# K of two heads as one transfer of 65536-byte rows, in a two-layer decode step with a KV cache of 16384 keys

## The chip, the cores and the metric

The kernel runs on one core of one Trainium2 chip. The metric is the device time of one execution in microseconds, lower is better. A core has five engines, each with its own instruction queue: TensorE (PE, with the weight load PEld shown apart), VectorE (DVE), ScalarE (ACT), GpSimd (POOL) and SyncE (SP). 16 DMA engines move data between the memory of the chip (DRAM) and the on-chip memory of 128 partitions. Matmuls write to a separate accumulator memory in banks (PSUM).

## The reference

Two times the same layer, one token for each of two batch rows: attention over a cache with 32 heads a row, 16384 keys, head size 128, then a small MLP with shifted channel groups. All inputs are bf16.

```python
def _A_ref(x, k_cache, v_cache, wq, wo):
    q = (x @ wq).reshape(B, Sq, H, Dh).transpose(0, 2, 1, 3)
    scores = jnp.einsum("bhqd,bhkd->bhqk", q, k_cache) * (Dh ** -0.5)
    p = _softmax(scores, axis=-1)
    o = jnp.einsum("bhqk,bhkd->bhqd", p, v_cache)
    return o.transpose(0, 2, 1, 3).reshape(B, Sq, H * Dh) @ wo
...
x = x + _A_ref(_layernorm(x), A_k_cache, A_v_cache, A_wq, A_wo)
x = x + _B_ref(_layernorm(x), B_w1, B_w2, B_w3, B_w4)
...
```

The last two lines run twice, with the same weights and the same cache. There are 2 x 32 = 64 heads, counted through as u = 0 to 63. K and V of a head are 16384 x 128 numbers of 2 bytes, 4 MiB each; a layer reads 64 of each.

## The kernel before, in words

**Memory.** K and V live in one tensor, `mem`, of six slots (`NSLOT`) of 32768 bytes a partition (`TILE`). A head's K fills one slot: partition p holds 128 keys in a row, so that the slot is 128 blocks, each with one key of every partition. A planner (`plan_all`, L516) writes down all transfers of the whole program in one order, each with its place in `mem`. `pump` (L289) hands the next one to SP as soon as all cells of its place are free; `used` (L1281) releases a place when its last reader is done. SP thus holds one list of transfers (issued at L101), and each waits at the head of the list for the release of its own place; all that are issued run one behind the other through the same DMA queue.

**What is transferred.** K comes head by head, 128 rows of 32768 bytes (`plan_tile`, L433). V of two heads comes as one transfer of 128 rows of 65536 bytes (`plan_pair`, L445): partitions 0 to 63 hold head u, partitions 64 to 127 head u + 1, in two neighbouring slots. In the loop of layer 0, K of the first head of a pair goes to slot 0, of the second to slot 2, and V of the pair to slots 4 and 5.

**One head.** A head's scores need each key times q. Half of the 128 blocks go by TensorE: in chunks of eight blocks, PE transposes them (L1298, `transposes`) into one of four PSUM tiles `tps`, ACT copies the chunk to one of three tiles `kt` (L1314, `evacuate`), and PE multiplies the eight blocks with the column of q (L1328, `scores`), two chunks behind. The other half goes by VectorE in four groups of 16 blocks: a multiply with q spread over the partitions (L1348) and a sum over the 128 elements (L1354), together `dots` (L1340). q is spread by a diagonal matrix (DVE, L1259), a matmul (PE, L1263) and a copy (ACT, L1266). Then the softmax: the maximum on DVE (L1363 to L1368), over the partitions on POOL (L1370), the scaling and two exponentials on ACT (L1379, L1382, L1385).

**One pair.** As V holds two heads, p of both heads is spread to V's layout, `both`, by two matmuls a head with a selecting matrix (L1418, `spread_p`) and a copy (L1424). Then 256 matmuls of a V block with two columns of `both` (L1455, `pv_pair`) give the outputs of both heads; ACT keeps them (L1459), and this releases the V place.

**Loops.** Each engine has its own hardware loop, made by `Graph._turn` (L235) from the instructions of the first turns: waits are rebased by a fixed step a turn (L265). A turn is one pair, two heads one after the other. Layer 0 loops over heads 1 to 60 (30 turns), layer 1 over 58 heads (29 turns); the heads ahead and behind are written out. A column that changes with the turn (the head's column of q or of the sums) is computed in a register from the turn's number:

```python
emit_op(eng, o, None if o.col is None else turn * (ops[first + n + i].col - o.col) + o.col)
```

All tiles of K and V are at the same places in every turn, so their addresses are constants. POOL tells PE and DVE that a transfer has landed (`relay`, L81 and L205).

**Between the layers** the output projection, the MLP and the next layer's q use the weights, which the planner puts in places left free; K of the last two heads of layer 0 stays in `mem`, transposed, for layer 1, which therefore starts with these heads. `turn` (L1109) and `park` (L1126) transpose blocks for that between other steps.

Of the kernel before, what the change touches and what calls it, by code (L numbers as in the profile page):

```python
# [5 lines left out]
ALU = mybir.AluOpType  # L6
# [10 lines left out]
class Op:  # L17


    __slots__ = ("eng", "fn", "deps", "waits", "needed", "own", "val", "sem", "sig", "col", "pos", "know", "relay", "told")  # L20

    def __init__(self, eng, fn, sig=None, col=None):
        self.eng, self.fn, self.sig, self.col = eng, fn, sig, col
# [9 lines left out]
class Graph:  # L33
# [44 lines left out]
    def op(self, eng, fn, reads=(), writes=(), sig=None, col=None):  # L78
        return self._add(Op(eng, fn, sig, col), reads, writes)
# [54 lines left out]
    def emit(self):  # L134
# [15 lines left out]
        for e in self.LOOPED:  # L150
            ops = self.ops[e]
            for first, (n, turns) in self.loops[e].items():
                for i in range(first, first + n):
# [8 lines left out]
                    if same[0].col is not None:  # L162
                        step = same[1].col - same[0].col
                        assert all(o.col == same[0].col + t * step for t, o in enumerate(same)), [o.col for o in same]
        done = {e: nc.alloc_semaphore(f"done_{e}") for e in self.ENGS if e != "sync"}
# [37 lines left out]
        def emit_op(eng, o, col=None):  # L203
# [3 lines left out]
            ins = o.fn(eng) if o.col is None else o.fn(eng, o.col if col is None else col)  # L207
# [27 lines left out]
    def _turn(self, eng, ops, first, n, turns, taken, wait, needs, emit_op, handle):  # L235
# [22 lines left out]
        with self.nc.Fori(0, turns, 1, engines=OrderedEngineSet([me]), head_slot={me: 0}) as turn:  # L258
            seen = {}
            for i in range(n):  # L260
                wait(eng, rel[i], seen)
                o = ops[first + i]
                emit_op(eng, o, None if o.col is None else turn * (ops[first + n + i].col - o.col) + o.col)
# [68 lines left out]
class KB:  # L332
# [8 lines left out]
    NS = 3  # L341
    DB = 16
    PB = 32
# [3 lines left out]
    ENTER = (1, 3)  # L347
    LEAVE = (61, 61)
    TURNS = {("w3", 0): 1, ("w3", 1): 1, ("w3", 2): 1, ("w4", 1): 1, ("w4", 3): 1, ("w4", 6): 1, ("w4", 8): 1,
             ("wq", 0): 1, ("wq", 1): 1, ("wq", 2): 1}  # L350

    def __init__(self, nc, A_x, K, V, wq, wo, w1, w2, w3, w4, out):
# [20 lines left out]
        self.chunk = 0  # L373
# [3 lines left out]
    def _alloc(self):  # L377
# [6 lines left out]
        self.same = sb("same", [128, 4, 128], BF16)  # L384
        self.ones_bf, self.ident, *self.sel = (self.same[:, i, :] for i in range(4))
        self.ones_f = sb("ones_f", [128, 1], FP32)
        self.diag = sb("diag", [128, 128], BF16)
        both = sb("both", [128, 4 * self.NB], BF16)
        self.both = both[:, :].rearrange("p (k c) -> p k c", k=2)
        self.qb = [both[:, 0:128]] + [sb(f"qb{i}", [128, 128], BF16) for i in range(1, self.NS)]  # L390
        self.p = [both[:, 128:128 + self.NB]] + [sb(f"p{i}", [128, self.NB], BF16) for i in range(1, self.NS)]
        self.both_keys = [("qb", 0), ("p", 0), ("p2", 0), "both"]
        self.s_dve = [sb(f"s_dve{i}", [128, 2 * (self.BP - self.PB)], FP32) for i in range(self.NS)]
        self.q_f = sb("q_f", [128, U], FP32)
        self.q_col = sb("q_col", [128, self.NS], BF16)
# [49 lines left out]
    def plan_pair(self, u, slot):  # L445

        v = self.V.rearrange("b h s d -> (b h s d)")
        n = self.NB * 128 * 128
        self.store.plan(("w", u, 0, 2 * self.NB), "pair", slot * self.TILE, 2 * self.TILE,
                        [(lambda m: m, v[u * n:(u + 2) * n].rearrange("(p x) -> p x", p=128))])  # L450
# [65 lines left out]
    def plan_all(self):  # L516
# [9 lines left out]
        third = U - self.CARRY - 1  # L526
# [6 lines left out]
        for t, u, slot in (("k", third, 1), ("k", third + 1, 3), ("v", third, 4), ("k", third + 2, 5),  # L533
# [1048 lines left out]
```

## Time and profile before

| what | value |
|---|---|
| runs of the kernel before | 2545.34, 2546.11, 2546.92 us (median 2546.11) |
| span of the profiled execution, its only own time | 2543.9 us |
| runs' median less that span | 2.2 us |
| bytes moved by the data queue | 1092.39 MB |
| mean rate over the span | 430 GB/s |

How to read the profile. Times are in microseconds from the start of the span. L1298 is line 1298 of the kernel. A row of the timeline or of the groups names the line, the engine, the operation, what it writes and reads (`out<-in`), and how often (`x8`); in square brackets stands how long the engine was idle before it and what ended that (`<-issue`: nothing that the profile shows). A row of the chain of waits is a start, a length and what ran; a row of waits is who waited, for whom, how long in all, how often, and the longest. An engine's name with a q (`PEldq`, `SPq`) is its sequencer: register, branch, semaphore and DMA-issuing instructions, which aren't counted as busy. The granted TensorE clock is a share of full speed.

### The profile page before, as it was taken

What the parts mean: (1) busy time and instruction counts of PE and PEld (TensorE: products, weight loads), DVE (VectorE), ACT (ScalarE), POOL (GpSimd) and SP (SyncE); (2) the same over time, 40 slices, a digit from 0 to 9 for tenths busy, and PEclk for the clock granted to TensorE, in tenths of its full rate; (3) what the DMA queues carried; (4) which work ended last, traced back from release to release, by engine and by line L of the source; (5) the groups of instructions that cost most, each with busy time, mean ns of one, the idle gap of its engine ahead of it and who ended that gap; (6) DMA issues with size and microseconds to landing.
All of it is one profiled execution on the core that took longest, in us unless ns stands there. A gap on an engine that the chain in (4) does not pass through costs nothing.

```text
span 2543.9 us, 75560 instructions
## 1 busy us (share of the span) xinstructions
PE 1588.5 (62%) x34642; PEld 1520.1 (60%) x34642; DVE 1875.3 (74%) x1811; ACT 1250.8 (49%) x2114; POOL 109.6 (4%) x154
## 2 busy tenths in 40 slices
PE   3656666566566566565776656656656666566566
PEld 3555656566565565565765656656556566566566
DVE  5787787777877877877748687787787787777884
ACT  3454555554544544545535455454454555554553
POOL 0000000000000000000000000000000000000000
PEclk8666665565656656666656566566666565665665
DMA  9999999999999999999999999999999999999999
GB/s 414 424 437 429 434 438 430 428 442 424 434 433 432 432 437 428 436 435 426 418 413 432 434 429 437 429 431 439 425 435 433 431 436 433 428 437 430 432 431 383
DMA packets 38432, 1093.19 MB, mean 430 GB/s; under 512 B 4196, under 2 KB 5352, under 8 KB 11496
## 3 DMA queue, kind: packets, MB, share of 16 engines
q1 hardware_dynamic: 38376, 1092.39, 99.9%
q8 instruction: 41, 0.67, 0.1%
q14 instruction: 15, 0.12, 0.0%
HBM read 1092.37 MB, written 0.00 MB: 429 GB/s over the span
## 4 chain that ended last, share of the span: by engine, by line
DMA 60%; DVE 27%; PE 7%; issue 4%; ACT 1%; POOL 0%; SPq 0%; POOLq 0%; DVEq 0%; ACTq 0%
DMA mem<-in_A_k_cache_dram 57%; DVE s_dve L1354 17%; DVE prod L1348 9%; PE tps L1298 3%; DMA mem<-in_B_w_dram 1%; DMA mem<-in_A_v_cache_dram 1%; PE mps L1482 1%; PE sps L1328 1%; PE sps L1263 1%; DVE diag L1259 1%; ACT mem L1314 0%; PE mps L897 0%; PE mps L1455 0%; DMA mem<-in_A_wq_dram 0%; DMA mem<-in_A_wo_dram 0%
## 5 line engine op out<-in xcount | busy, mean ns | idle before, releaser
L1354 DVE TENSOR_REDUCE s_dve<-prod 128x16 f32<-128x2048 bf16 x504 | 1151.1, 2284 | 13.3
L1314 ACT ACTIVATE kt<-tps 128x1024 bf16<-128x1024 bf16 x992 | 966.5, 1029 | 171.8 <-PE tps L1298 159.9
L1348 DVE TENSOR_TENSOR prod<-mem,qb 128x2048 bf16<-128x2048 bf16 x492 | 602.1, 1224 | 524.5 <-POOLq L205 490.6
L1298 PE MATMUL tps<-same,mem 128*128 128x128 bf16 x8192 | 910.7, 285 | 31.3 <-issue 24.6
L1298 PEld LDWEIGHTS tps<-same,mem 128*128 128x128 bf16 x8192 | 730.8, 130 | 37.2 <-issue 30.2
L1455 PEld LDWEIGHTS mps<-both,mem 128*128 128x128 bf16 x15104 | 407.5, 103 | 48.2 <-ACT both L1424 43.2
L1455 PE MATMUL mps<-both,mem 128*128 128x2 bf16 x15104 | 412.5, 165 | 32.6 <-ACT both L1424 27.8
L1328 PE MATMUL sps<-q_col,kt 128*128 128x1 bf16 x7936 | 364.6, 168 | 53.6 <-ACT kt L1314 44.9
L1328 PEld LDWEIGHTS sps<-q_col,kt 128*128 128x128 bf16 x7936 | 351.7, 108 | 74.2 <-ACT kt L1314 69.6
L1418 PE MATMUL sps<-p,same 128*128 128x128 bf16 x236 | 46.3, 299 | 481.2 <-ACT p L1385 481.2
L1418 PEld LDWEIGHTS sps<-p,same 128*128 128x128 bf16 x236 | 15.6, 111 | 491.2 <-ACT p L1385 491.2
L1263 PE MATMUL sps<-diag,same 128*128 128x128 bf16 x126 | 36.0, 286 | 286.4 <-DVE diag L1259 284.6
L1370 POOL PARTITION_ALL_REDUCE mx<-mx x128 | 106.5, 832 | 2366.3 <-DVE mx L1368 2259.0
L1459 ACT ACTIVATE o_acc<-mps 128x2 f32 x59 | 10.2, 172 | 383.7 <-PE mps L1455 383.7
L1263 PEld LDWEIGHTS sps<-diag,same 128*128 128x128 bf16 x126 | 13.1, 104 | 296.8 <-DVE diag L1259 290.1
L1379 ACT ACTIVATE mx<-mx 128x1 f32<-128x1 f32 x128 | 26.2, 205 | 332.1 <-POOL mx L1370 332.0
L1266 ACT ACTIVATE qb<-sps 128x128 bf16<-128x128 f32 x123 | 33.8, 275 | 228.1 <-PE sps L1263 228.1
L1424 ACT ACTIVATE both<-sps 64x256 bf16<-64x256 f32 x118 | 44.6, 378 | 57.2 <-PE sps L1418 57.2
L1365 DVE TENSOR_REDUCE mx<-sps 128x1 f32<-128x64 f32 x128 | 28.2, 220 | 23.2 <-PE sps L1328 23.1
L1382 ACT ACTIVATE p<-s_dve,mx 128x64 bf16<-128x64 f32 x123 | 42.8, 348 | 4.0
L1314 ACT ACTIVATE mem<-tps 128x1024 bf16<-128x1024 bf16 x32 | 31.3, 1044 | 18.1 <-PE tps L1298 16.0
L1430 ACT ACTIVATE l<-ls 128x1 f32 (+1 forms) x120 | 35.3, 294 | 9.0
(131 smaller groups left out, 460.5 us busy)
## 6 DMA issues: line engine op xcount, KB each, us to landing
mem<-in_A_k_cache_dram SPq DMA_DIRECT2D x124, 4096.0 KB, 24.0
mem<-in_A_v_cache_dram SPq DMA_DIRECT2D x5, 4096.0 KB, 29.7
mem<-in_B_w_dram SPq DMA_DIRECT2D x21, 576.0 KB, 7.8
mem<-in_B_w_dram SPq DMA_DIRECT2D x7, 1152.0 KB, 32.7
mem<-in_A_v_cache_dram SPq DMA_DIRECT2D x3, 2048.0 KB, 36.9
mem<-in_A_wq_dram SPq DMA_DIRECT2D x10, 512.0 KB, 6.5
mem<-in_A_wo_dram SPq DMA_DIRECT2D x8, 576.0 KB, 18.4
mem<-in_A_wq_dram SPq DMA_DIRECT2D x4, 1024.0 KB, 8.0
```

The source lines that it names most:

```text
L1263: self.pe(lambda pe: pe.matmul(qps, lhsT=self.ones_bf[:, :], rhs=self.diag[:, :], start=True, stop=True, skip_group_check=True), reads=["o ...
L1298: ins = pe.transpose(self.tps[t][:, j * 128:(j + 1) * 128], buf[:, j * 128:(j + 1) * 128], self.ident[:, :])
L1314: self.act(lambda e: e.activation(out=out, in_=self.tps[t][:, :], func=ACT.Copy), reads=[("tps", t)], writes=keys, sig=("evac", c, t, k))
L1328: ins = pe.matmul(self.sps[sp][:, c * self.CH + j:c * self.CH + j + 1], lhsT=buf[:, j * 128:(j + 1) * 128], rhs=self.q_col[:, sp:sp + 1], ...
L1348: self.dv(lambda e: e.tensor_tensor(out=prod, in0=buf.rearrange("p (j d) -> p j d", d=128), in1=qbc, op=ALU.mult), reads=[("qb", r)] + key ...
L1354: self.dv(lambda e: e.tensor_reduce(out=sd[:, c0:c0 + DB], in_=prod, axis=AX.X, op=ALU.add), reads=["prod"], writes=[("s_dve", r)], sig=(" ...
L1370: self.pool(lambda e: e.partition_all_reduce(mx[3], mx[2], channels=128, reduce_op=ROP.max), reads=[("mx2", i), "cleared"], writes=[("mx3" ...
L1382: self.act(lambda e: e.activation(out=p[:, n:self.NB], in_=self.s_dve[i][:, 0:self.NB - n], func=ACT.Exp, bias=mx[4], scale=self.scale, ac ...
L1418: ins = pe.matmul(out[:, h * n:(h + 1) * n], lhsT=lhsT, rhs=self.p[i][:, :], start=True, stop=True, skip_group_check=True)
L1424: self.act(lambda e: e.activation(out=self.both[lo:hi, k, :], in_=out[lo:hi, :], func=ACT.Copy), reads=[("sps", 0), ("qps", 0)], writes=se ...
L1430: self.act(lambda e, c: e.activation(out=self.l[:, bass.ds(c, 1)], in_=self.ls[:, 0, i:i + 1], func=ACT.Identity, bias=self.ls[:, 1, i:i + ...
L1455: ins = pe.matmul(self.mps[:, 448:450], lhsT=buf[:, b * 128:(b + 1) * 128], rhs=self.both[:, :, col], start=b == 0, stop=b == 2 * self.NB ...
```

## The change

K of two heads is now planned as one transfer too, with the layout of V. `plan_pair` takes K or V:

```diff
-    def plan_pair(self, u, slot):
-        v = self.V.rearrange("b h s d -> (b h s d)")
+    def plan_pair(self, t, u, slot, cuts=()):
+        v = (self.K if t == "kp" else self.V).rearrange("b h s d -> (b h s d)")
...
-        self.plan_tile("k", 0, 1)
+        self.plan_tile("k", 0, 2)
         self.plan_tile("v", 0, 3)
-        for u in range(1, third, 2):
-            self.plan_tile("k", u, 0)
-            self.plan_tile("k", u + 1, 2)
-            self.plan_pair(u, 4)
...
+        place = lambda i: 0 if i % 2 else 2
+        self.plan_pair("kp", o[1], place(1))
+        for i in range(2, n + 1):
+            self.plan_pair("kp", o[2 * i - 1], place(i))
+            self.plan_pair("vp", o[2 * i - 3], 4)
```

The K places alternate: pair 1 in slots 0 and 1, pair 2 in slots 2 and 3, and so on; V pairs are always in slots 4 and 5. The order of the queue is K1, K2, V1, K3, V2, K4 and so on (Ki and Vi: pair i). There are 30 pairs in layer 0 and 29 in layer 1 (`PAIRS`); the first of each layer is written out, the others are the turns of the loop (29 and 28).

Since the place alternates, an operation can have an address that depends on the turn's parity. `Graph._turn` puts it into a register, and the operation adds its own offset:

```diff
+                if o.alt is not None:
+                    k = (o.alt, then.alt)
+                    if k not in flips:
+                        lo, d = min(k), abs(k[1] - k[0])
+                        flips[k] = self.nc.snap(((turn + (1 if k[0] > lo else 0)) % 2) * d + lo,
+                                                engines=OrderedEngineSet([me]))
+                    alt = flips[k]
...
+    def pair_transposes(self, l, u, k, c, at):
...
+                ins = pe.transpose(self.tps[t][:, j * 128:(j + 1) * 128],
+                                   self.mem[:, bass.ds(base + (c * self.CH + j) * 128, 128)], self.ident[:, :])
```

The same is done for the multiplies of `pair_dots`. A turn (`pair`) now is:

```diff
+    def pair(self, l, u, k, prev):
+        self.landed("kp", u, both=True)
+        pend = []
+        n = self.NB // self.CH
+        for c in range(n):
+            at, self.chunk = self.chunk, self.chunk + 1
+            self.pair_transposes(l, u, k, c, at)
+            spot = self.kt_spot(at)
+            self.evacuate(at, spot)
+            pend.append((c, spot))
+            if len(pend) > self.LEAD:
+                self.pair_scores(*pend.pop(0))
+            if c % 2 == 0:
+                self.pair_dots(l, u, k, c // 2)
+            if prev is not None and c == self.MID:
+                self.landed("vp", prev)
+            if prev is not None and self.MID <= c < self.MID + 2:
+                for g in range(2):
+                    self.pv_pair_part(l, prev, 2 * (c - self.MID) + g)
+            if prev is not None and c == self.MID + 1:
+                self.keep_pair(l, prev)
+        for c, spot in pend:
+            self.pair_scores(c, spot)
+        self.pair_max()
+        self.q_turn(u + 2)
+        self.pair_exp(u)
+        for nm in self.store.pieces("kp", u):
+            self.store.release(nm)
```

So 16 chunks a pair are transposed (128 of the pair's 256 blocks), `pair_scores` multiplies each block with two columns (q of both heads), and eight groups of 16 blocks go by DVE (`pair_dots`). The scores of a pair are in one PSUM bank and one tile `s_dve`, with a head in each half of the partitions. `pair_max` takes the maximum of each half (five DVE operations, one all-reduce of two columns on POOL); `pair_exp` writes the exponentials straight into `both`: two scalings, four exponentials and two kept sums on ACT. The last kept sum also stands as the last reader of the K place, which is released there. `spread_p` is gone, and so is the diagonal: q is spread by two matmuls with a repeated column of q (`rows_of_q`). PV of the previous pair (`pv_pair_part`, four parts of 64 matmuls) comes inside the pair, after chunks 12 and 13 (`MID` = 12), instead of at its end.

Around the loops: the heads not in pairs (one ahead in layer 0, three behind it in each layer) run through `single`, with the same steps as before but all DVE groups in the second half of the blocks. Layer 1 takes the carried heads in the order 61, 62, 63 and then 0 to 60. The last head of layer 0 takes its chunks in the order 5, 6, 7, 3, 4, 0, 1, 2, so that its last key chunks stay where they were transposed (`kt` and `tps`) for layer 1, in place of `park`. The bytes loaded are the same.

More of the change, by code (lines that the diff above doesn't have):

```diff
@@ L1083, in attention @@
[L1083 to L1086 removed]
+            self.q_row(o[0], 0, 2)
+            self.q_turn(o[1], None)
+            self.single(o[0], 0, 2)
+            self.softmax_max(o[0], 0, 2)
+            self.softmax_exp(o[0], 0, 2)
+            self.pv(l, o[0], 0)
+        self.pair(l, o[at(1)], 0, None)
+        first = self.g.mark()
+        self.base = self.chunk
+        for i in range(2, n + 1):
+            self.pair(l, o[at(i)], (i - 1) % 2, o[at(i - 1)])
```

785 lines of the change are left out of this document (357 added, 428 removed).

## The prediction

> **What bounds the kernel now.** I read the page's head first, for the resource that never rests.
>
> ```profile
> span 2543.9 us, 75560 instructions
> ...
> PE 1588.5 (62%) x34642; PEld 1520.1 (60%) x34642; DVE 1875.3 (74%) x1811; ACT 1250.8 (49%) x2114; POOL 109.6 (4%) x154
> ...
> q1 hardware_dynamic: 38376, 1092.39, 99.9%
> ```
>
> The transfers fill 99.9% of the span; no engine passes 74%. Who waits for whom comes next, from two answers on waits: that of SyncE's queue and that of all engines.
>
> ```profile
> SPq L101 <- PE sps L1328: 1577.9, 120, 41.9
> SPq L101 <- ACT o_acc L1459: 683.3, 59, 37.5
> ```
>
> ```profile
> DVE prod L1348 <- POOLq L205: 490.6, 58, 9.8
> ```
>
> SP issues each transfer as soon as its place is released and runs ahead of the DMA engines. VectorE waits for the landing of K in every turn: 490.6/58 = 8.5 us a turn. The stream of K and V is the bound, and compute has slack. How much, the windows show: four that reach from the first packet of one transfer to that of the next kind (V pair, K and K, V pair, K and K), then one whole turn. Columns: window, its length, busy time of PE, PEld, DVE, ACT, POOL, TensorE's granted clock, DMA share, GB/s.
>
> ```profile
> 598.59:617.95 19.36, 8.29 (x134) 8.11 (x132) 18.97 (x16) 9.80 (x16) 1.31 (x1) 0.66 1.01 438
> 617.95:637.38 19.43, 15.84 (x397) 15.12 (x394) 10.32 (x12) 9.76 (x19) 0.35 (x1) 0.55 1.00 430
> 637.38:656.72 19.34, 7.72 (x124) 7.46 (x125) 18.95 (x16) 9.49 (x16) 1.31 (x1) 0.71 1.00 434
> 656.72:676.15 19.43, 15.66 (x397) 14.64 (x395) 10.32 (x12) 9.75 (x19) 0.35 (x1) 0.58 0.99 427
> 591.30:630.08 38.78, 24.31 (x523) 23.54 (x521) 29.29 (x26) 19.52 (x33) 1.66 (x2) 0.59 1.00 433
> ```
>
> A turn of two heads is 38.78 us, the time of 16.78 MB at 433 GB/s. In it PE is busy for 24.31 us and DVE for 29.29. The chain of waits gives the pieces.
>
> ```profile
> 4.63 22.79 DMA mem<-in_A_k_cache_dram
> ...
> 591.32 1.24 DVE prod L1348
> 592.58 2.30 DVE s_dve L1354
> 594.90 1.24 DVE prod L1348
> ...
> 603.80 0.85 PE tps L1298 x8
> 604.65 0.20 PE sps L1328 x8
> ```
>
> One dot group costs DVE 594.90 - 591.32 = 3.58 us, eight of them 28.6; one transpose 0.85/8 = 0.106 us.
>
> **The change, part by part.**
>
> *K as one transfer of 65536-byte rows.* Bytes stay. The windows price it: the V pair, which has this form already, takes 19.34 to 19.36 us, the same bytes as two K transfers 19.43. So 0.07 to 0.09 us a pair, I take 0.08; with 30 + 29 pairs 4.7 us less (4.1 to 5.3). The windows' GB/s stand farther apart (438 and 434 against 430 and 427), but a window's edge cuts packets, and one packet of 65536 B is 0.8% of it; the lengths count. As the stream is 99.9% full, this is all that can be gained.
>
> *Dots, scores, softmax.* Eight dot groups a turn as before, so DVE keeps 28.6 us; 128 transposes, 16 evacuations and 256 PV matmuls stay too. The timeline at a turn's end has the rest:
>
> ```profile
> 621.00 0.22 DVE L1365 TENSOR_REDUCE mx<-sps 128x1 f32<-128x64 f32 x1 [0.28 <-PE sps L1328]
> 621.26 0.16 DVE L1368 TENSOR_TENSOR mx<-mx 128x1 f32<-128x1 f32 x1
> ...
> 621.51 0.35 POOL L1370 PARTITION_ALL_REDUCE mx<-mx  x1 [6.78 <-DVE mx L1368]
> 621.90 0.20 ACT L1379 ACTIVATE mx<-mx 128x1 f32<-128x1 f32 x1 [1.36 <-POOL mx L1370]
> 622.13 0.35 ACT L1382 ACTIVATE p<-s_dve,mx 128x64 bf16<-128x64 f32 x1
> ...
> 622.92 0.39 PE L1418 MATMUL sps<-p,same 128*128 128x128 bf16 x2 [1.96 <-ACT p L1385]
> 623.35 0.38 ACT L1424 ACTIVATE both<-sps 64x256 bf16<-64x256 f32 x1 [0.48 <-PE sps L1418]
> 623.75 0.72 ACT L1430 ACTIVATE l<-ls 128x1 f32 x2
> ...
> 623.78 6.99 PE L1455 MATMUL mps<-both,mem 128*128 128x2 bf16 x256 [0.47 <-ACT both L1424]
> ```
>
> Gone: twice the spread (0.39 on PE, 0.38 on ACT), the diagonal and one all-reduce of two. New at the pair's end: five DVE steps (about 1.0 us), one all-reduce (0.35), two scalings (0.4), four exponentials (1.4), two sums kept (0.72): 3.9 us from the last dot to the release of the K place. PE's next pair waits there after two chunks, because the scores have one bank. All of it lies beside the stream as long as a turn of compute stays under 38.7 us: DVE 28.6 + 1.0, then 2.9 for the rest, is 32.5. It costs nothing while 6 us of cover last.
>
> *Addresses from a register.* The place alternates between turns, so each of the 128 transposes, and each of the eight multiplies, gets its K address from a register. No row of before shows a register-addressed transpose. Nearest rows: the loop's own register and semaphore instructions on PE's sequencer (all of them, then three in a window of one back edge; minimum, median, maximum ns, first and last start):
>
> ```profile
> L258 PEldq ALU_OP  x59: 36/36/42, 92.6 to 2464.2; - x59
> ...
> L265 PEldq EVENT_SEMAPHORE  x3: 51/51/51, 591.4 to 591.7; - x3
> ```
>
> Three semaphore instructions of 51 ns start over 0.3 us, 0.15 apart. Scaled by 36/51, a register operation holds the sequencer for 0.106 us. A load and its matmul pass in 6.99/256 = 0.027. Lower bound of a transpose: the 0.106 of today, with the register work hidden ahead of the array. Upper: 0.15 + 0.027 = 0.18; if load and matmul are both slowed, or two operations are needed, above 0.2. I take 0.106 + 0.027 = 0.133, nearest to the ALU row. PE's turn then is 128 x 0.133 = 17.0, scores 16 x 0.20 = 3.2, PV 7.0, and about 6 for the pair's end (3.9 plus the last evacuations, 1.03 each): 33 us, under 38.7. PE becomes the bound at (38.7 - 16.2)/128 = 0.176 us a transpose. The eight on DVE are below 8 x 0.15 = 1.2 us and inside the slack.
>
> The Trainium skill speaks against this part: "TensorE: Matmul & The Clock Gate", section "Step-by-step: what each phase is for", says that a matmul not handled by the hardware decoder takes the sequencer about 62 ns. No run here shows whether a register address has that effect; 0.027 us for a PV pair says that plain ones don't. By it, as an estimate, a transpose would be 0.106 + 0.124 = 0.23 us and the second rival below would hold.
>
> *The queue at each layer's start.* K of pair i+2 waits for the end of pair i; V of pair i waits for PV of pair i-1, which now stands after chunk 12 of 16 of pair i. In the steady turn the V place is free some 10 us before its slot in the queue. Not at pair 2, where the loops start. Rows: entry of the first loop on DVE and ACT, and of the second on PE.
>
> ```profile
> 50.32 1.23 DVE L1348 TENSOR_TENSOR prod<-mem,qb 128x2048 bf16<-128x2048 bf16 x1 [6.49 <-issue]
> ...
> 54.61 1.94 ACT L1314 ACTIVATE kt<-tps 128x1024 bf16<-128x1024 bf16 x2 [5.24 <-PE tps L1298]
> ```
>
> ```profile
> 1349.76 1.46 PE L1298 MATMUL tps<-same,mem 128*128 128x128 bf16 x12 [4.97 <-issue]
> ```
>
> Layer 0: the first K lands at 4.63 + 22.79 = 27.4; V of that head 9.7 later; then pair K1, K2, V1, K3 at 19.35 each: K1 at 56.5, K3 ends at 114.5. Pair 1 computes from 56.6: 28.6 of dots, about 1 of gaps, 3.9 of end: 90. ACT's entry (5.2): 95. Then a chunk each 8 x 0.133 + 0.25 = 1.31 us: chunk 12 at 111, PV in two halves with a chunk between 8.3, o kept and V2 issued: 120, first bytes about 1 later. The stream stands for 121 - 114.5, about 6.5, and with the evacuations of chunks 0 and 1 behind the stall, 8 us. Bounds: nothing, if the entry is not waited for and a chunk stays at 1.1; 13 at 0.18 a transpose. Layer 1 is built alike, with a costlier entry on PE: 9. Both are paid once; after them the queue has its slack again.
>
> *The rest* (q rows made without the diagonal, tiles kept where they are transposed, layer order) changes engines with slack, beside the stream: nothing, at most 1 us either way.
>
> Sum on the profiled execution: 2543.9 - 4.7 + 8 + 9 = 2556.2; the median of the runs is 2.2 above that span, so **2558.4**.
>
> **Rivals.**
>
> *The start holes are covered (not slower).* Register work hides in the 0.106 us and the entry stalls fall into waits for K2: V2 is issued before 113.5, the stream stays full, and only the 4.7 remain: 2541.4 (2540.8 to 2542). It decides at whether PV of pair 1 ends before K3's last packet. For it: 24.31 us of PE in 38.78. Against: the 5.24 and 6.49 us rows.
>
> *PE's sequencer becomes the bound.* From 0.176 us a transpose on, the turn follows PE. At 0.20: 16.2 + 25.6 = 41.8, 3.1 over, in 29 + 28 looped turns 177 us: 2558.4 + 177 = 2735; at 0.18 2587; at 0.23, 2950. For it: 0.15 us between sequencer instructions, 128 of them new. Against: a sequencer may run ahead of the array while PE waits.
>
> *The rows bring nothing* (the DMA engines already hide what lies between packets; the 0.08 us is K's own place in the memory): the holes alone, 2563.
>
> *A fixed price per transfer falls away.* If each transfer's end cost 2 us of the stream, 59 fewer would give 118: 2428. Against it: 19.43 for two K and 19.35 for one V; an end costs 0.08. The rule is that of the Trainium skill, "SBUF — State Buffer", section "The DMA setup-cost knee", where every transfer pays about 2 us and larger ones are advised; by those two rows the trace doesn't bear it out for transfers queued back to back.
>
> **How the numbers follow.** Forecast 0.42 (2548 to 2580), covered 0.24, PE-bound 0.27, no gain 0.05, fixed price 0.02. A measurement of this kernel can tell about 0.2%, 5.1 us. Faster than 2541.0: half of the covered case and more, and the fixed price: 0.16. Within: the rest of the covered case and the lower end of the forecast, 0.15. Slower: 0.69. The range, 2539 to 2730, leaves out the fixed price, a little below, and PE-bound turns over 0.2 us a transpose. The forecast's own range is 2548 to 2580.
>
> **What would show it.** Right: V-pair issues 38.69 us apart instead of 38.78; the DMA tenths full except for one hole of 5 to 12 us near 115 us and one behind the layer change; DVE still waiting about 6 us a turn for K; transposes in chunks of 8 over 1.0 to 1.1 us; register rows on PE, 128 a turn. Wrong: DMA share under 98% all along with DVE or ACT waiting for PE (second rival); no hole (first); windows of K still 19.43 long (third). The forecast falls most easily with the one number that no row shows, a register-addressed transpose.

## The result and the profile after

| | before | after |
|---|---|---|
| median of the runs | 2546.48 us (2545.34 to 2546.92, 4 runs) | 2561.65 us (2559.45 to 2563.38, 4 runs) |
| span of the profiled execution | 2543.9 us | 2561.1 us |
| ratio, 95% interval | | 1.0059 (1.0044 to 1.0073) |

The change makes the kernel slower by 15.2 us; 2558.4 was forecast. The page of the kernel after, in the rows that answer to those shown of before:

```profile
span 2561.1 us, 82046 instructions
...
PE 1629.7 (64%) x34370; PEld 1472.1 (57%) x34370; DVE 1881.2 (73%) x1550; ACT 1255.4 (49%) x1944; POOL 31.1 (1%) x95
...
DMA  9899999999999999999999999999999999999999
GB/s 412 379 441 427 438 430 437 431 428 440 426 441 427 441 427 440 428 439 428 378 390 423 412 426 440 428 440 428 438 430 435 433 430 438 426 442 426 442 424 387
...
q1 hardware_dynamic: 30024, 1092.39, 99.2%
```

The same bytes, the queue 99.2% full instead of 99.9%, and three places where the rate falls under that of before: the second slice of 64 us (379, before 424), the twentieth and twenty-first, where the layers meet (378 and 390, before 418 and 413), and the twenty-third, where the loop of layer 1 starts (412, before 434). In the loops nothing is lost. SP's rows in the timeline of the kernel after (start, length, what is issued) give the steady turn from V pair to V pair:

```profile
344.37 0.33 SPq L101 DMA_DIRECT2D mem<-in_A_v_cache_dram  x1
...
383.07 0.33 SPq L101 DMA_DIRECT2D mem<-in_A_v_cache_dram  x1
```

383.07 - 344.37 = 38.70 us, against 38.78 before. The answer on waits shows that VectorE still waits for K in nearly every turn, 395.1/55 = 7.2 us each time:

```profile
DVE prod L1309 <- POOLq L206: 395.1, 55, 14.3
```

Where the loss sits is seen best by bytes. From the records of all packets I worked out the time at which each trace had moved a given number of megabytes, and took before from it. A number that grows down a column is time that the stream lost there, one that shrinks is time won. (e11, whose turns are longer, is not in the table.)

| trace | 45 MB | 60 MB | 520 MB | 575 MB | 650 MB | 1050 MB | 1092 MB |
|---|---|---|---|---|---|---|---|
| (place) | start | behind pair 2 | end of loop 0 | layer change over | behind pair 2 | end of loop 1 | end |
| after | -0.6 | 7.0 | 5.1 | 14.3 | 19.2 | 17.3 | 17.8 |
| e1 | -0.5 | 1.8 | 0.1 | 6.0 | 9.1 | 7.2 | 8.2 |
| e2 | -0.4 | -0.2 | 0.0 | 9.3 | 11.9 | 9.9 | 12.9 |
| e3 | -0.4 | 7.2 | 7.2 | 15.7 | 21.0 | 20.8 | 22.0 |
| e4 | -0.6 | 5.3 | 3.7 | 7.5 | 9.9 | 7.9 | 9.7 |
| e5 | -0.6 | 5.8 | 4.1 | 14.3 | 15.6 | 13.7 | 18.1 |
| e6 | -0.6 | 6.8 | 4.6 | 14.5 | 19.3 | 17.5 | 17.8 |
| e7 | -0.6 | 8.6 | 6.7 | 15.1 | 21.8 | 19.9 | 22.2 |
| e8 | -0.6 | -0.4 | -2.3 | 8.4 | 8.4 | 6.5 | 11.4 |
| e9 | -0.5 | 6.7 | 4.5 | 14.0 | 19.0 | 17.1 | 17.2 |
| e10 | -0.7 | -0.5 | -2.4 | 6.8 | 6.7 | 4.8 | 4.9 |
| e12 | -0.6 | -0.4 | -2.3 | 1.4 | 1.8 | -0.1 | 0.0 |

The row "after" is the whole story: 7.6 us lost at the start of layer 0, 1.9 won back in its loop, 9.2 lost at the layer change (0.9 near 1243 us, 5.4 near 1275, 3 where layer 1's first loads begin), 4.9 at the start of layer 1, 1.9 won back.

Each row is one execution, the profiled one, and that is not always a typical one: e1's took 2552.84 us (five runs of 2552.84 to 2560.77, median 2557.23), e2's 2557.76 (eleven runs of 2551.28 to 2557.76, median 2554.36). And the layer change costs between 3.8 us (e4) and 10.2 (e5) in versions whose instructions there are the same as in the kernel after. So a row places a loss, but two rows that differ by two or three microseconds show no difference by themselves.

Three windows of the kernel after show it as rate (the last columns are TensorE's clock, DMA share and GB/s; 433 is full):

```profile
100.00:130.00 30.00, 23.53 (x486) 20.69 (x485) 22.53 (x19) 17.04 (x29) 0.35 (x1) 0.61 0.76 319
...
1240.00:1280.00 40.00, 29.02 (x757) 27.80 (x758) 16.44 (x16) 14.40 (x23) 0.50 (x2) 0.59 0.88 353
1400.00:1420.00 20.00, 12.62 (x290) 11.19 (x286) 16.89 (x15) 6.52 (x18) 0.37 (x1) 0.50 0.81 333
```

The hole of layer 0 in the timeline of the kernel after (idle time before an instruction and its releaser in brackets):

```profile
89.79 0.60 ACT L1351 ACTIVATE l<-mq 64x1 f32<-64x1 f32 x2
90.41 0.33 SPq L101 DMA_DIRECT2D mem<-in_A_k_cache_dram  x1
...
95.73 12.95 ACT L1386 ACTIVATE kt<-tps 128x1024 bf16<-128x1024 bf16 x13 [5.35 <-issue]
...
110.47 3.26 PE L1363 MATMUL mps<-both,mem 128*128 128x2 bf16 x117 [2.37 <-issue]
...
115.71 3.55 PE L1363 MATMUL mps<-both,mem 128*128 128x2 bf16 x128
...
119.40 0.17 ACT L1372 ACTIVATE o_acc<-mps 128x2 f32 x1 [2.68 <-PE mps L1363]
119.60 0.33 SPq L101 DMA_DIRECT2D mem<-in_A_v_cache_dram  x1
```

It runs in the order that the prediction wrote: pair 1 ends at 90.4, ACT enters the loop with 5.35 us of nothing, 13 chunks follow at 1.0 us (forecast 1.31), PV of pair 1 with the chunk between its halves takes 11.6 us (107.67 to 119.26, forecast 8.3, with two stops of PE in it), and V2 is issued at 119.60 (forecast 120). In layer 1 the same place looks so:

```profile
1385.84 0.60 ACT L1351 ACTIVATE l<-mq 64x1 f32<-64x1 f32 x2
1386.46 13.00 ACT L1386 ACTIVATE kt<-tps 128x1024 bf16<-128x1024 bf16 x13
...
1405.78 0.27 PE L1286 MATMUL tps<-same,mem 128*128 128x128 bf16 x1 [3.03 <-issue]
...
1411.58 0.33 SPq L101 DMA_DIRECT2D mem<-in_A_v_cache_dram  x1
```

ACT enters its second loop without a wait. From the end of pair 1 to the issue of V2 it takes 1411.58 - 1386.46 = 25.1 us, in layer 0 119.60 - 90.41 = 29.2. The difference is 4.1 and not 5.35, because PE's stops by "issue" are longer here (3.03 and 1.47 us against 2.37 and 0.89).

At the layer change the last head of layer 0 (K lands at 1246.3) is late. Rows of the kernel after:

```profile
1243.34 0.17 ACT L1372 ACTIVATE o_acc<-mps 128x2 f32<-128x2 f32 x1 [7.11 <-PE mps L1363]
...
1243.54 2.77 SPq L101 DMA_DIRECT2D mem<-in_A_v_cache_dram  x4
...
1246.38 1.23 DVE L1406 TENSOR_TENSOR prod<-mem,qb 128x2048 bf16<-128x2048 bf16 x1 [12.49 <-DMA mem<-in_A_k_cache_dram]
1246.58 2.94 PE L1468 MATMUL mps<-p,mem 128*128 128x1 bf16 x105 [2.17 <-issue]
...
1274.66 0.23 DVE L1043 CAST prod<-sps 128x64 bf16<-128x64 f32 x1 [0.33 <-PE sps L1039]
```

And two of the kernel before, the first multiply of its last head and the last step of its attention:

```profile
1240.87 1.23 DVE L1348 TENSOR_TENSOR prod<-mem,both 128x2048 bf16<-128x2048 bf16 x1 [0.17 <-DMA mem<-in_A_k_cache_dram]
...
1263.93 0.22 DVE L1107 CAST prod<-sps 128x64 bf16<-128x64 f32 x1 [0.33 <-PE sps L1103]
```

From the landing of the last K to the end of attention it took 23.1 us before and takes 28.3 now. Behind that K stand V of b and c (2 x 9.7 us) and five pieces of the output weights (5 x 1.36 us): 26.2 us. SP issues the sixth piece when PE has begun the output projection; the kernel before, then the kernel after:

```profile
1264.93 0.33 SPq L101 DMA_DIRECT2D mem<-in_A_wo_dram  x1
```

```profile
1275.67 0.33 SPq L101 DMA_DIRECT2D mem<-in_A_wo_dram  x1
```

Before, this was 24.1 us behind the landing of the last K, with bytes still queued; now it is 29.4, the stream has run dry 3.2 us earlier, its next bytes come some time behind the issue, and 5.4 us are lost. Of the 5.2 us by which the way to the end of attention grew, most are stops of PE by "issue": 2.17, 1.88 and 0.73 us behind the landing of the last K, 4.8 in all, against 0.6 before.

### The profile page after: what moved, and what is told of

Read it like the earlier page. It is cut to its first block, busy times and chain, and to the rows that moved or that the text cites. A ratio compares the mean times of both kernels' runs of the same rounds, so it can differ in the third digit from the quotient of the medians.

```text
span 2561.1 us, 82046 instructions
## 1 busy us (share of the span) xinstructions
PE 1629.7 (64%) x34370; PEld 1472.1 (57%) x34370; DVE 1881.2 (73%) x1550; ACT 1255.4 (49%) x1944; POOL 31.1 (1%) x95
## 3 DMA queue, kind: packets, MB, share of 16 engines
q1 hardware_dynamic: 30024, 1092.39, 99.2%
## 4 chain that ended last, share of the span: by engine, by line
DMA 73%; PE 20%; DVE 3%; issue 2%; ACT 1%; SPq 1%; ACTq 0%; POOLq 0%; DVEq 0%
DMA mem<-in_A_v_cache_dram 66%; PE mps L1363 16%; DMA mem<-in_A_k_cache_dram 4%; PE tps L1286 3%; DVE s_dve L1312 1%; DMA mem<-in_B_w_dram 1%; SPq L101 1%; DVE prod L1309 1%; PE sps L1297 1%; DMA mem<-in_A_wq_dram 1%; PE mps L1468 1%; ACT o_acc L1372 0%; DMA mem<-in_A_wo_dram 0%; PE sps L1395 0%; PE mps L925 0%
## 5 line engine op out<-in xcount | busy, mean ns | idle before, releaser
L1386 ACT ACTIVATE kt<-tps 128x1024 bf16<-128x1024 bf16 x989 | 998.0, 1025 | 810.3 <-PE tps L1286 782.3
L1286 PE MATMUL tps<-same,mem 128*128 128x128 bf16 x7552 | 941.9, 260 | 359.7 <-POOLq L206 351.6
L1312 DVE TENSOR_REDUCE s_dve<-prod 128x16 f32<-128x2048 bf16 x472 | 1078.9, 2286 | 16.2
L1286 PEld LDWEIGHTS tps<-same,mem 128*128 (+1 forms) x7552 | 693.9, 108 | 483.2 <-issue 357.8
L1309 DVE TENSOR_TENSOR prod<-mem,qb 128x2048 bf16<-128x2048 bf16 x472 | 577.9, 1224 | 457.0 <-POOLq L206 395.1
L1297 PE MATMUL sps<-q_pair,kt 128*128 128x2 bf16 x7552 | 336.4, 167 | 49.9 <-ACT kt L1386 48.5
L1297 PEld LDWEIGHTS sps<-q_pair,kt 128*128 128x128 bf16 x7552 | 316.0, 104 | 62.5 <-ACT kt L1386 58.2
L1372 ACT ACTIVATE o_acc<-mps 128x2 f32 (+1 forms) x59 | 10.2, 172 | 168.6 <-PE mps L1363 168.6
L1270 PE MATMUL tps<-same,mem 128*128 128x128 bf16 x600 | 64.7, 285 | 6.3 <-POOLq L206 3.9
L1328 DVE TENSOR_REDUCE mq<-sps 64x1 f32<-64x128 f32 x118 | 34.0, 288 | 46.9 <-PE sps L1297 45.0
L1270 PEld LDWEIGHTS tps<-same,mem 128*128 128x128 bf16 x600 | 53.4, 131 | 6.8 <-POOLq L206 4.1
L1468 PE MATMUL mps<-p,mem 128*128 128x1 bf16 x1280 | 36.7, 165 | 20.7 <-ACT p L1436 11.0
L1468 PEld LDWEIGHTS mps<-p,mem 128*128 128x128 bf16 x1280 | 35.7, 103 | 22.0 <-ACT p L1436 11.3
L1342 ACT ACTIVATE both<-s_dve,mq 64x128 bf16<-64x128 f32 x118 | 47.1, 399 | 2.2
```

The lines of the kernel that those rows point to most:

```text
L1270: ins = pe.transpose(self.tps[t][:, j * 128:(j + 1) * 128], buf[:, j * 128:(j + 1) * 128], self.ident[:, :])
L1286: ins = pe.transpose(self.tps[t][:, j * 128:(j + 1) * 128], self.mem[:, bass.ds(base + (c * self.CH + j) * 128, 128)], self.ident[:, :])
L1297: ins = pe.matmul(self.sps[1][:, i:i + 2], lhsT=buf[:, j * 128:(j + 1) * 128], rhs=self.q_pair[:, :], start=True, stop=True, skip_group_ch ...
L1309: self.dv(lambda e, base: e.tensor_tensor(out=prod, in0=self.mem[:, bass.ds(base + b * 128, DB * 128)].rearrange("p (j d) -> p j d", d=128 ...
L1312: self.dv(lambda e: e.tensor_reduce(out=self.s_dve[2][:, d * DB:(d + 1) * DB], in_=prod, axis=AX.X, op=ALU.add), reads=["prod"], writes=[( ...
L1328: self.dv(lambda e, h=h, r=r: e.tensor_reduce(out=m[r, 1:2], in_=self.pair_scored(r, h), axis=AX.X, op=ALU.max), reads=[("sps", 1)], write ...
```

## The experiments

Theory A: the steady turn is as forecast, and all losses lie at the layers' starts (PV of pair 1 ends too late for V2) and ends (TensorE's and ScalarE's work ahead of the last head). Rivals: the register addresses slow the turns; the rows of 65536 bytes bring nothing; code loading alone is the loss. Medians are against 2546.7 to 2546.9 us of the kernel before on the same chips.

**e1, pair 2 written out** (`MID2` = 12).

```diff
         self.pair(l, o[at(1)], 0, None)
+        self.pair(l, o[at(2)], 1, o[at(1)], self.MID2)
...
-        for i in range(2, n + 1):
+        for i in range(3, n + 1):
...
-        self.g.loop(first, n - 1)
+        self.g.loop(first, n - 2)
```

> The changed kernel with pair 2 of each layer written out ahead of the loop, PV of pair 1 still after its chunk 12; the loops begin at pair 3. The changed kernel stood 15.2 us over before; its transfers fall behind by 7.6 us near 110 us and by 4.6 near 1405 us. Theory A (both parts count: the loop entry of some 5 us on ACT and PE, and the place of PV): the hole of layer 0 shrinks by about 5 us, to 2 to 3; 8 to 10 us over before. Rival B (the place of PV alone): holes as they were, 15 us over before. Rival C (the entry alone): both holes gone, 3 us over.

Measured: 2557.23 us (2552.84 to 2560.77), ratio 1.0043 (1.0030 to 1.0057), 10.3 over. By the bytes the hole of layer 0 is 2.3 us instead of 7.6; that of layer 1, where ACT had no entry stall, 3.1 instead of 4.9. That is theory A: the entry cost 5 us of the hole, the place of PV the rest. A pair that is written out also has constant K addresses, which could be the cause instead; rows of this run separate the two:

```profile
90.42 12.26 ACT L1389 ACTIVATE kt<-tps 128x1024 bf16<-128x1024 bf16 x13
...
112.72 1.26 PE L1366 MATMUL mps<-both,mem 128*128 128x2 bf16 x42 [3.10 <-issue]
```

ACT starts at 90.42 instead of 95.73, 5.3 us earlier, and its 13 chunks take 12.26 us instead of 12.95, so the addresses are worth 0.7 at most. Stops of PE by "issue" remain in the code that is written out.

**e2, and PV of pair 1 after chunk 4** (`MID2` = 4).

> As the run before it, and in the written-out pair 2 PV of pair 1 comes after chunk 4 instead of 12, which is 8 chunks of 1.04 us earlier. Theory A and rival B: both holes go, 12 us less than the changed kernel, 3 us over before. If the holes have another cause (the release of the K place, for one): 10 to 15 us over before.

Measured: 2554.36 us (2551.28 to 2557.76), 1.0026 (1.0017 to 1.0036), 7.4 over instead of 3. V2 is issued at 107.74, and at 60 MB nothing has been lost. But the loop now begins at pair 3, and 2.3 us go there, between 60 and 70 MB (2.6 in layer 1): V3 is issued at 153.65, 45.9 us behind V2. I read it as the same wait, met one pair later.

**e3, K of a pair in two transfers.**

```diff
-                            [(lambda m: m, src[:, a * 128:z * 128])])
+                            two if t == "kp" and z - a == 2 * self.NB else [(lambda m: m, src[:, a * 128:z * 128])])
```

with `two` the left and the right half of the same rows.

> The changed kernel with K of a pair loaded as two transfers of 32768-byte rows into the same place (those in one piece; the pieces of layer 1's first pair stay). Theory A (rows of 65536 bytes bring 0.08 us a pair): a turn goes back from 38.70 to 38.78 us, 4.5 us more than the changed kernel, 19.7 over before. Rival (the rows bring nothing, the gain was of the places): turns stay 38.70, 15.2 over before. Rival of a fixed price per transfer (2 us): 58 more transfers, 116 us more.

Measured: 2563.37 us (2562.47 to 2566.33), 1.0063 (1.0050 to 1.0077). The median is only 1.7 above that of the changed kernel, with intervals that overlap; the trace decides. SP's rows:

```profile
422.45 0.33 SPq L101 DMA_DIRECT2D mem<-in_A_v_cache_dram  x1
430.51 0.80 SPq L101 DMA_DIRECT2D mem<-in_A_k_cache_dram  x2
461.24 0.33 SPq L101 DMA_DIRECT2D mem<-in_A_v_cache_dram  x1
```

461.24 - 422.45 = 38.79 us: the gain of the turn is gone, and in the table the columns 60 to 520 and 650 to 1050 MB stand still (7.2, 7.2; 21.0, 20.8). One transfer of long rows instead of two of short ones brings 0.08 to 0.09 us a pair, and a transfer more costs no more than that, not 2 us. The place is the same in both, so the gain is not the place's. Whether the longer rows or the one transfer fewer bring it is not separated: e3 changes both.

**e4, transposes of a constant block.**

```diff
-                                   self.mem[:, bass.ds(base + (c * self.CH + j) * 128, 128)], self.ident[:, :])
+                                   self.ident[:, :], self.ident[:, :])
```

> The changed kernel with the 128 transposes of a pair reading the constant identity tile at a fixed address instead of K at the address in the register: no register operation on PE. It leaves out the scores of half of the keys in the paired heads (they are made from the identity). Theory A (the register work is beside the stream): a transpose goes from 0.124 to 0.106 us, the time stays within 3 us of the changed kernel, 12 to 16 over before; at most the holes shrink by 1.5 each. Rival (the sequencer is what makes the loop late): 5 us or more less, turns below 38.70.

Measured: 2552.66 us (2550.38 to 2557.44), 1.0024 (1.0014 to 1.0033), 9.0 less than the changed kernel. Theory A gave at most 3; the rival's 5 or more came with turns below 38.70 us, and they stay (V issued at 614.53 and 653.23). So the turns are not it: loops 0 and 1 win 1.6 and 2.0 us by the bytes, as in the changed kernel. The holes shrink by 1.7 and by 2.5, and 5.4 go at the layer change, whose instructions the edit does not touch. There, PE's groups from 1240 to 1285 us show less idle time by "issue"; the kernel after, then this run:

```profile
L1468 PE MATMUL mps<-p,mem 128*128 128x1 bf16 x384 | 11.2, 165 | 4.8 <-issue 2.9 <-ACT p L1436 1.1 <-POOLq L206 0.6
L1270 PE MATMUL tps<-same,mem 128*128 128x128 bf16 x96 | 10.2, 288 | 2.4 <-issue 1.9 <-ACT kt L1386 0.5
```

```profile
L1468 PE MATMUL mps<-p,mem 128*128 128x1 bf16 x384 | 11.2, 166 | 2.8 <-ACT p L1436 1.1 <-POOLq L206 0.9 <-issue 0.5
L1270 PE MATMUL tps<-same,mem 128*128 128x128 bf16 x104 | 9.0, 256 | 0.6 <-ACT kt L1386 0.6
```

2.9 + 1.9 us became 0.5, and from the landing of the last K to the end of attention it takes 25.0 us (1244.94 to 1269.89) instead of 28.3. Without the register operations the loop's code is shorter, so that the code behind it stands elsewhere; that this moves the stops is likely, but it was not tested by itself.

**e5, PV after chunk 10 in every pair** (`MID = 10`).

> The changed kernel with PV of the previous pair after chunk 10 of every pair instead of 12. Theory A (the start holes last until PV of pair 1 is done): V2 is issued two chunks, 2.1 us, earlier, the hole of layer 0 shrinks from 7.6 to 5.5 us, that of layer 1 from 4.6 to 2.5; turns stay 38.70; 11 us over before. Rival (PE then waits longer for V in each turn and the pair's end slips past the landing of the next K): turns over 38.70 us, each 0.1 us of it 5.7 us in all.

Measured: 2559.67 us (2557.96 to 2562.61), 1.0046 (1.0033 to 1.0060), 13.0 over where 11 was expected. The holes are 6.4 and 1.3 us; the loops win as before. At the end of layer 1, 4.4 us are lost (1050 to 1092 MB) where the changed kernel loses 0.5 and other versions with the old order there up to 3.0 (e2).

**e6, the last head's exponentials ahead of PV of b.**

```diff
         self.softmax_max(c, 0, 2)
-        self.pv(l, b, 1)
         self.softmax_exp(c, 0, 2)
+        if l:
+            self.pv(l, b, 1)
...
-            self.single(c, 0, 2, order=(5, 6, 7, 3, 4, 0, 1, 2))
+            self.single(c, 0, 2, order=(5, 6, 7, 3, 4, 0, 1, 2), before={5: lambda: self.pv(l, b, 1)})
```

> The changed kernel with another order behind the loops alone: PV of head b comes inside the last head's chunks in layer 0 (before its sixth) and behind that head's exponentials in layer 1, so that ACT isn't held by the kept output of b ahead of the exponentials of the last head. Theory A (the hole of 5.4 us near 1275 us is the end of the last head's chain: 27.9 us from the landing of its K to the end of attention, against 23.1 before, with 26 us of transfers queued behind that K): the chain shortens by 4 to 5 us, the hole goes to 0 to 1.5; 10 us over before. Rival (it is code loading or the clock in straight-line code, which the order doesn't change): hole 3 to 6 us, 13 to 16 over before.

Measured: 2563.69 us (2561.41 to 2565.04), 1.0063 (1.0050 to 1.0077), 17.0 over where theory A gave 10 and its rival 13 to 16. Nothing gained: the chain is 28.7 us. My reading of it falls: PE itself is the bound there. The timeline of this run shows PV of b pushing the last head's remaining chunks back, and three of its four waits by "issue" (4.7 us in all):

```profile
1253.46 3.68 PE L1271 MATMUL tps<-same,mem 128*128 128x128 bf16 x33 [1.88 <-issue]
...
1258.72 3.44 PE L1469 MATMUL mps<-p,mem 128*128 128x1 bf16 x128
...
1266.23 0.44 PE L1396 MATMUL sps<-q_b,kt 128*128 128x1 bf16 x9 [0.66 <-issue]
...
1273.47 0.46 PE L1469 MATMUL mps<-p,mem 128*128 128x1 bf16 x12 [1.08 <-issue]
```

**e7, one register step more a transpose.**

```diff
+                at = base + (c * self.CH + j) * 128
+                if not isinstance(at, int):
+                    at = self.nc.snap(at, engines=OrderedEngineSet([pe.engine]))
...
-                                   self.mem[:, bass.ds(base + (c * self.CH + j) * 128, 128)], self.ident[:, :])
+                                   self.mem[:, bass.ds(at, 128)], self.ident[:, :])
```

> The changed kernel with each transpose's address put into a register of its own first, so that it takes one more register operation. By the prediction's sum (PE's turn 16.2 us + 128 times a transpose, bound at 0.176): a transpose of 0.124 + 0.08 to 0.10 = 0.20 to 0.22 us makes turns of 42 to 45 us and 180 to 350 us more than the changed kernel. Rival (the sequencer runs ahead while PE waits, so that the threshold lies higher): turns stay within 1 us of 38.7, less than 60 us more.

Measured: 2566.40 us (2563.97 to 2566.92), 1.0072 (1.0057 to 1.0088), 4.8 more than the changed kernel and not 180 or more. The step didn't make a second operation but a longer one. PE's register rows by line, of the kernel after, then of this run (minimum, median, maximum ns):

```profile
L1286 PEldq FUSED_REGOPS  x7239: 46/46/46, 87.8 to 2450.2; - x196
```

```profile
L1288 PEldq FUSED_REGOPS  x7239: 102/103/103, 87.8 to 2454.8; - x196
```

The pace within a chunk, from the starts of the matmuls, goes from 0.124 to 0.181 us, so 0.078 us beside the register operation in both. By the chunk (its 1.49 us less 0.22 for the eight matmuls of its scores) it is 0.159, under the 0.176 of the prediction, and the turns stay 38.70. It only makes the holes longer: 9.2 and 6.7 us.

**e11, two steps more** (a second such line, with `at + 128`, and 128 taken off in the operand).

> The changed kernel with two more register steps for each transpose's address. In e7 one more step made one register operation of 103 ns instead of 46 and a pace of 0.181 us a transpose within a chunk (0.159 by the chunk, since the sequencer runs ahead during the scores). Two more: some 160 ns, a pace of 0.24, 0.21 to 0.22 by the chunk. By the prediction's sum, 16.2 + 128 x 0.215 = 43.7 us a turn, 5.0 over the 38.7 of the transfers: 285 us more than the changed kernel (150 to 420). Rival (the threshold of 0.176 is wrong, since 16.2 counted waits that the sequencer uses): turns under 41 us.

Measured: 2735.80 us (2735.70 to 2735.89), 1.0741 (1.0721 to 1.0760), 174 more than the changed kernel. Register operations of 158 ns; the page and SP's rows:

```profile
PE 2410.6 (88%) x34370; PEld 1553.9 (57%) x34370; DVE 1881.6 (69%) x1550; ACT 1262.7 (46%) x1944; POOL 31.1 (1%) x95
...
q1 hardware_dynamic: 30024, 1092.39, 94.2%
```

```profile
623.69 0.33 SPq L101 DMA_DIRECT2D mem<-in_A_v_cache_dram  x1
...
665.10 0.33 SPq L101 DMA_DIRECT2D mem<-in_A_v_cache_dram  x1
```

Turns of 41.41 us: this is the second rival made real. The pace within a chunk is 0.236 us, the register operation of 0.158 plus 0.078 again. A chunk takes 1.93 us, less 0.22 for its scores 0.214 a transpose; 16.2 + 128 x 0.214 gives 43.6, so the part beside the transposes is 14.0 us, not 16.2, and by this sum PE becomes the bound at (38.7 - 14.0)/128 = 0.193 us. The granted clock was 0.52 in e7 and e11 and 0.64 in the kernel after, so the 14.0 us are those of the lower clock.

**e8, e1's loop with PV after 4 and 10, and e6's ends.**

> Pair 2 written out with PV of pair 1 after chunk 4, PV after chunk 10 in the loop, and the order of e6 behind the loops. Theory A (the losses are the start holes and the end of each layer's attention, nothing in the steady turn): both start holes go (12.2), the 2.3 and 1.9 us that were left at pair 3 in e2 go, the hole near 1275 goes (5): 0 to 3 us below before. If something of the steady state is lost by the earlier PV: over before.

Measured: 2553.76 us (2552.39 to 2555.76), 1.0025 (1.0015 to 1.0035), 7.1 over where 0 to 3 below was expected. The start holes are gone in both layers (columns 45 to 60 and 575 to 650), and at the end of loop 0 the stream is 2.3 us ahead of before. The ends lose 10.7 and 4.9 us. The second is seen in this run's timeline:

```profile
2480.94 0.16 DVE L1425 TENSOR_TENSOR mx<-mx 128x1 f32<-128x1 f32 x1
2481.21 5.10 PE L1367 MATMUL mps<-both,mem 128*128 128x2 bf16 x185 [3.62 <-POOLq L206]
2488.50 2.05 PE L1367 MATMUL mps<-both,mem 128*128 128x2 bf16 x71 [2.19 <-issue]
```

PV of the last pair waits for POOL, which tells PE of the landing only behind b's maximum (by the packets, that V had landed at 2472.5); V of b waits for that PV's place.

**e9, another order at the ends.**

```diff
-        self.single(b, 1, 1, still=l == 0, after={...})
+        self.single(b, 1, 1, still=l == 0, before={3: lambda: self.pv_pair(l, last)}, after={...})
...
         self.softmax_exp(b, 1, 1)
-        self.pv_pair(l, last)
...
             self.pv(l, a, 0)
-            self.turn(4)
...
-        self.pv(l, b, 1)
         self.softmax_exp(c, 0, 2)
+        self.pv(l, b, 1)
```

and the four chunks of that `turn` beside the output projection.

> The changed kernel with another order behind the loops alone: PV of the last pair stands inside head b (before its fourth chunk) instead of behind b's softmax; the second four of the transposes for layer 1 go beside the output projection of layer 0 instead of ahead of the last head; the last head's exponentials stand ahead of PV of b on ScalarE. Theory A (at a layer's end the bound is TensorE's list of work, 30 us of it behind the landing of the last K: PV of the last pair, PV of a, four chunks for layer 1, code loading): V of b is issued 5 us or more earlier, the end of attention comes 4 to 6 us earlier, and the 0.9 and 5.4 us that the transfers lost near 1243 and 1275 us shrink to 0 to 2; 9 to 11 us over before. Rival (the loss is code loading of straight-line code, which the order doesn't change): 14 us or more over before.

Measured: 2562.25 us (2561.61 to 2564.30), 1.0060 (1.0047 to 1.0074), 15.4 over: theory A gave 9 to 11, its rival, code loading, 14 or more. V of b is issued at 1235.85 instead of 1243.54 and the 0.9 us are gone, but the other loss grew to 7.6. The timeline of this run names the next in line:

```profile
1245.48 3.77 ACT L1384 ACTIVATE mem<-tps 128x1024 bf16<-128x1024 bf16 x4 [1.34 <-PE tps L1268]
...
1250.33 0.26 ACT L1232 ACTIVATE qb<-sps 128x128 bf16<-128x128 f32 x1
1250.62 1.23 DVE L1404 TENSOR_TENSOR prod<-mem,qb 128x2048 bf16<-128x2048 bf16 x1 [5.60 <-ACT qb L1232]
```

The last head's dots wait 5.60 us for its q, which ACT copies behind the other four chunks for layer 1 and b's exponentials.

**e10, e9's ends with e8's starts.**

> The order of e9 behind the loops, and pair 2 written out with PV of pair 1 after chunk 4, and PV after chunk 10 in the loops. Theory A (all losses lie at the layers' starts and ends): start holes gone, end of layer 0 some 2 us ahead of before, 3 us lost at the layer change, 2 won in layer 1, and the 5 us that e8 lost near 2487 us gone because PV of the last pair no longer waits behind b's maximum on POOL: 3 us below to 2 over before. If the ends stay as in e8: 7 over.

Measured: 2551.86 us (2550.65 to 2554.40), 1.0019 (1.0010 to 1.0028), 5.0 over where at most 2 was expected. The end of layer 1 loses nothing more; the layer change still 9.2.

**e12, q of the last head first, no chunk for layer 1 ahead of it.**

```diff
+        self.q_row(c, 0, 2)
         self.softmax_max(b, 1, 1)
-        if l == 0:
-            self.turn(4)
         self.softmax_exp(b, 1, 1)
```

with four of the eight chunks beside the output projection and the rest as in the kernel before.

> As e10, and behind the loops q of the last head is spread ahead of b's softmax, and none of the eight chunks for layer 1 stands ahead of the last head: four go beside the output projection, one more beside the gate product, three beside the next layer's q as in the kernel before. e10 lost 6.4 us near 1268, where the last head's first multiply waited for its q until 2.7 us after K had landed and ScalarE was copying those chunks. Theory A (the loss is what stands ahead of the last head on PE and ACT): dots of the last head start with the landing, the end of attention comes 24 to 25 us after it, the loss goes to 0 to 1.5: 5 us less than e10, 1 below to 2 over before. Rival (code loading of the written-out code, 2 us a piece): the loss stays 4 us or more.

Measured: 2547.18 us (2546.10 to 2548.34), 1.0002 (0.9993 to 1.0011): no difference from before, 14.5 less than the changed kernel and, each against the kernel before on its own chip, 4.6 less than e10. The first multiply of the last head and the end of attention:

```profile
1240.20 1.23 DVE L1405 TENSOR_TENSOR prod<-mem,qb 128x2048 bf16<-128x2048 bf16 x1 [2.81 <-DMA mem<-in_A_k_cache_dram]
...
1264.96 0.23 DVE L1041 CAST prod<-sps 128x64 bf16<-128x64 f32 x1 [0.33 <-PE sps L1037]
```

The chain is 1264.96 - 1240.2 = 24.8 us, and 2.3 us are lost near 1268 (0 to 1.5 expected) where e10 lost 6.4. Both loops win their 1.9 us, and 3.7 at the layer change take them back. No version here beats the kernel before.

## Why the prediction was right, and where its steps were off

- **Bound by the stream, the rows 4.7 us.** Right. Turns of 38.70 us; in e3 the loops no longer win it. The bytes show 0.6 + 1.9 + 1.9 = 4.4 us won.
- **A register-addressed transpose, 0.133 us, hidden beside the stream.** Right: 0.124 (register operation 0.046, not 0.106; 0.078 beside it, not 0.027 - two errors that cancel). The 62 ns a matmul that the Trainium skill ("TensorE: Matmul & The Clock Gate", section "Step-by-step: what each phase is for") gives for matmuls outside the hardware decoder would have made 0.23 us, as an estimate; the pace of 0.124 speaks against that for register addresses.
- **PE the bound from 0.176.** Nearly: 0.193 by the sum of e11. The rival of PE as the bound was real, at a register operation three times as long.
- **The start of layer 0, 8 us.** Right, 7.6, by the mechanism that it named: e1 shows 5 for the entry, e2 the rest. That the issue of V2 came within 0.4 us was luck in part: 13 chunks at 1.0 us instead of 1.31 let PV begin 3.3 us early (107.67, forecast 111), and PV with its two stops took 3.3 longer than its 8.3.
- **The start of layer 1, 9 us.** Oversized: 4.9. The step took a first entry on ACT once more and a dearer one on PE (the 4.97 of before); in the kernel after ACT's second entry cost nothing and PE's 0.55, while stops of 3.03 and 1.47 us came in the turn.
- **"The rest ... at most 1 us either way".** This step failed: 9.2 us at the layer change. It called tiles kept transposed and layer order work of engines with slack. That is true of the loop; at a layer's end the stream has only 26 us of transfers left behind the last K, and everything that PE and ACT do ahead of the last head counts, with the stops of PE among it. The change put PV of the last pair, q of the last head and eight chunks for layer 1 there. e9 moved part of it and uncovered the next, e12 the rest: 9.2 became 3.7. e4 has all of that work in its old place and loses 3.8, with 4.3 us less of stops; so the loss is work and stops together.

The total came out near by luck: the missed loss of 9 and the oversized start of layer 1 by 4 partly cancel, and the runs' medians stand 15.2 apart where the two profiled spans stand 17.2 apart.

Open: what is left of the layer change in e12 (3.7 us), and what decides whether a load of code stops PE there: in e4, with the same instructions, only 0.5 us of stops fall behind the last K.

## What to carry to other kernels

When a stream is 99.9% full, a better transfer shape can win only its own difference per transfer, here 0.08 us in 38.78, and any change of order is priced by the holes that it makes where a loop starts and where it ends. Look there for each transfer that must wait for a consumer, ask what bytes are queued behind it, and follow that consumer's engine lists back. A loss at such a place is a chain: moving one piece out shows the next, so budget for the whole list of work ahead of it.

## What the runs showed of the hardware

- A register-addressed weight load keeps the pace of its register operation plus 0.078 us: 46, 103 and 158 ns gave 0.124, 0.181 and 0.236 us a transpose within a chunk, at granted clocks of 0.64, 0.52 and 0.52. By the chunk it is less in the last two, 0.159 and 0.214: the first register operation of a chunk is done while the matmuls of the scores still run (in e11 one at 602.75, with the scores from 602.78 to 603.18).
- Entering a loop for the first time cost ACT 5.35 us with nothing to wait for, the second loop nothing. In first turns and in code that is written out PE stopped for 0.7 to 3.1 us at a time while the data queue was full. The profile calls this "issue"; the records of the packets tie it to the loading of code. The page of the kernel after counts the packets of the instruction queue q8:

```profile
q8 instruction: 49, 0.80, 0.1%
```

Each has 16384 bytes. PE stopped 16 times by "issue" for 0.8 us or more, 28.2 us in all, and 14 of these stops end 1.26 to 1.53 us after such a packet has landed; the other two come where the first turn of each loop goes over into the second. In the kernel before it is 10 of 10 (25.2 us, 1.25 to 1.59 behind a landing). This rests on times alone; no run changes the loading by itself. ACT's 5.35 us end 1.43 us after a packet of 8192 bytes of another instruction queue, in e4 too. Most loads stop nothing, and stops alone are not the loss: e12 has more of them than the kernel after (22, 43.4 us) and stands level with the kernel before. They cost where the stream waits for what PE or ACT does next.
